# Attention and a gated MLP on one core: another written order of all operations, and another choice of engine for the movable ones

## The chip, the cores and the metric

The kernel runs on one core of a Trainium2 chip. Five instruction streams run side by side on that core: TensorE (PE, with its weight loads shown as PEld), VectorE (DVE), ScalarE (ACT), GpSimd (POOL) and SyncE (SP), which issues most of the DMAs. Each stream takes its own instructions strictly in the order in which they are written, and the streams wait for each other at semaphores. The metric is the device time of one execution in microseconds (us). Three runs of the kernel before gave a median of 943.7 us (943.67 to 944.27).

## The reference

Batch 8, 8 heads, 576 queries, head width 64. Keys and values are averaged over groups of 8 positions, so that 72 keys are left, and after the attention an MLP with a sigmoid gate runs over 4608 tokens.

```python
k_p = k.reshape(B, H, Sp, 8, D).mean(axis=3)      # Sp = 72
v_p = v.reshape(B, H, Sp, 8, D).mean(axis=3)
scores = scale * q @ k_p^T ; scores -= max
attn = exp(scores) / (sum(exp(scores)) + 1e-9)
x = (attn @ v_p), heads side by side              # 4608 x 512
h = x @ w_in                                      # 4608 x 2048
g = h * sigmoid(1.702 * h)
out = g @ w_out                                   # 4608 x 512
```

All inputs and the output are float32.

## The kernel before

**Work.** A batch's 576 tokens are cut into a chunk of 512 and 64 left over; the left-over tokens of all 8 batches make a ninth chunk (c = 8), gathered through DRAM. Batch b's attention makes the input of chunk b. Per batch: DMA keys and values, pool them on DVE (`red`, `kbd`, `vbd`, L747, L889), bring the queries in transposed 32-blocks (`qr`, `qt`), scores on PE (`sps`, L1148), maximum and subtraction on DVE (`nm`, `sc`, L1171, L1179), exp on ACT (L1200), sums and weighting (L1205, L1221), then the weights are rearranged by small copies of 32 rows (`tail` L1262, `main` L1271) and block transposes (`mt`, `tt`), split in a high and a low part (`ah`, `al`), and multiplied with the values (`pav`, L1406 to L1409). `pav` is copied to the chunk's `x` and to `xt` (L1448, L1451, L1460).

**Stages of the MLP.** At the start the weights come in as raw words and are decoded (`raw`, `e`, `w`, L1586 to L1633) into a high and a low float32r half. Chunks 0 and 1 are computed densely (`h`, L1693 to L1695; `g`, `gh`, `gl`, L1710 to L1723; `o`, L1735 to L1737). Chunks 2 to 8 use a seven-product form of a 2x2 block product, in f16 pieces: for each of 8 pairs p of hidden tiles the banks `ha` and `hb` take seven products (L1982), ACT and DVE copy, add and gate them (L1997, L2005, L2017), and the gated tiles are split into `gh` and `gl` (L437/L440 and L2043, or on POOL L2048 and L2051).

**The fold.** That form needs other weights. While chunk 1 runs, `fold` renews both weights: high and low half are added (L1774, tiles `stage` and `shared`), scaled (L437 on ACT or L440 on DVE, tile `t`), added and subtracted against each other (L1818, tile `stage`), and cut into an f16 high part (L1756) and the rest (L1759). The first weight's pieces go to DRAM (`wd`) and come back pair by pair (`ws`); the second's stay in place (`t1`).

**What sets the order.** The kernel first records every operation as a task, with its engine, what it reads and what it writes, and nothing is issued. Many tasks are movable: a copy may run on ACT or DVE, a SBUF-to-SBUF sum on POOL or DVE; a task then carries both forms. At the end a table of 4871 numbers, `ORDER`, is read from left to right; each number is the place of a task in the record, a negative one (-n-1) means that the task is issued on its other engine:

```python
for n in map(int, ORDER.split()):
    t = tasks[n if n >= 0 else -n - 1]
    if n < 0:
        t.swap()
    t.emit()
```

DMAs are tasks too, so the table also sets the order of SP's queue. The waits at semaphores follow from what the tasks read and write.

Of the kernel before, what the change touches and what calls it, by code (L numbers as in the profile page):

```python
# [42 lines left out]
3 0 2074 2075 2076 2077 2078 2079 2080 2081 2082 2083 2084 11 169 170 171 10 162 163 4 31 164 73 172 165 12 7 -168 32  # L43
-169 176 177 6 5 25 178 179 26 27 72 8 2 1 45 50 33 166 34 51 46 204 205 206 -182 23 24 52 47 35 2085 17 228 9 14 13
36 53 48 49 54 207 2086 183 184 185 29 40 41 30 37 38 229 230 231 42 43 39 44 2087 2088 2089 2090 155 57 156 157 55
173 65 16 15 18 19 20 21 68 56 58 67 66 59 60 64 74 97 61 63 62 -76 182 208 158 186 159 160 187 161 180 98 190 191 77
-77 69 -79 70 99 82 83 192 100 101 212 209 213 214 -175 22 107 84 102 -104 85 197 108 198 92 79 2091 87 104 88 112 215
28 -81 81 -94 86 199 451 268 252 449 220 300 244 308 448 284 450 456 236 260 457 292 324 276 458 340 459 418 417 416
415 316 269 270 109 89 105 271 106 94 113 253 254 90 114 255 117 91 110 95 221 96 115 111 116 232 175 200 193 2094
2095 2096 2097 2098 2099 2100 2101 188 189 222 194 223 -203 -196 216 203 2092 2109 2110 2111 2112 2113 2114 2115 119  # L50
2102 2103 2104 245 201 118 120 121 122 127 128 246 196 123 124 2116 -130 2107 136 130 125 -132 -138 247 -211 126 -212
2108 2105 2117 2118 218 237 238 261 138 132 2106 2119 2120 239 224 139 262 135 217 226 233 -134 134 219 2124 142 2122
2125 2126 -142 140 263 277 278 -235 -236 279 240 227 248 225 143 309 310 249 2127 2128 2129 148 144 2130 2131 2132
2133 -150 -243 301 302 280 -146 311 -251 -148 452 146 2123 150 303 264 2134 2218 2219 2220 421 151 152 422 285 286 287
419 2221 2121 2222 2223 2224 2225 293 241 294 295 2226 2227 312 251 243 -267 -268 272 256 -259 -260 71 288 2135 2136
2137 2139 2140 2141 2142 2143 2144 2145 2146 2228 2138 341 342 281 265 257 372 348 364 356 388 -154 460 343 420 -283
-284 428 427 429 430 332 296 325 273 326 2147 2148 313 327 2093 2229 425 2230 2233 2234 2235 2236 2237 2238 2239 2231
426 2240 2149 298 299 328 -275 2152 453 2232 2150 297 357 358 359 275 2151 317 2241 318 -2243 314 333 319 454 -291 433
466 464 473 396 467 472 475 465 434 474 404 431 432 334 289 -316 -2244 335 344 360 291 468 455 2154 2155 2156 2157
2158 2153 2159 2160 469 2248 2249 2161 2250 2251 2252 2244 2253 2254 435 470 304 306 -308 471 2162 329 -2164 336 305  # L60
2164 349 350 -331 476 351 2245 461 2255 2246 462 365 366 320 -323 463 367 2247 352 331 345 2256 2257 346 446 2165 477
2169 2170 2171 2172 2173 2174 2175 2166 2176 2167 2168 523 518 516 439 515 438 380 603 154 526 517 525 524 321 353 373
-324 436 447 478 -348 479 2258 374 2177 375 -339 -2179 424 389 390 -363 391 440 480 481 482 337 368 339 2179 2259 2261
2263 2264 2265 2266 2267 2268 2269 2180 2181 2182 2270 2260 405 361 406 407 483 519 527 441 442 2184 2183 376 363 2185
2186 2187 2188 2189 2190 2191 2271 2272 381 382 541 589 532 539 534 604 540 531 533 588 392 437 -445 445 2273 377 484
2262 486 487 489 383 -355 485 488 490 2274 2276 2278 2279 2192 2193 520 2280 355 -379 -380 384 370 397 398 521 522
2275 497 2281 399 535 2282 2277 -499 423 499 2194 393 385 -395 2293 536 537 2294 2295 2296 2283 491 2284 2285 2286
2195 395 2197 -493 493 538 -372 528 2297 494 2287 369 644 641 642 542 643 605 606 386 495 543 529 443 530 400 2288 387
408 409 402 2199 2200 2201 503 2202 496 -505 505 544 545 645 546 547 2203 2204 2291 506 2298 2299 2300 2205 2206 509
2292 2198 2196 590 -411 -404 411 401 2207 2208 2209 -511 511 548 -508 508 2289 512 2290 513 500 501 2301 2302 549 2308  # L70
2309 2310 2311 2214 514 552 550 502 551 2215 553 2312 2303 558 607 -560 560 412 556 554 654 592 639 591 2306 2304 2313
2314 2210 2315 565 2211 2323 2316 2317 593 555 -567 567 557 2324 561 2307 2325 2326 2327 2328 572 562 594 -2319 563
587 -565 -574 574 619 613 637 612 638 610 620 611 568 2321 -596 598 571 599 609 -570 575 -579 570 608 576 577 2329
2330 2331 601 2305 2342 579 413 636 -2333 -2334 2343 2319 2353 2354 -581 614 616 581 615 -601 582 2322 583 2338 2344
2320 2334 584 640 -2527 -598 414 602 585 2216 596 617 2335 2212 2339 2345 2355 2356 -619 2346 2347 646 2348 621 658
659 651 625 652 624 656 657 653 2357 2336 2358 2340 647 -2528 649 648 623 650 622 -635 -2547 660 2550 2530 -2532 655
626 627 2359 2364 2365 2366 2367 2352 2350 2351 2349 2360 661 662 -2548 2537 -2539 663 629 -2549 2368 2369 2536 2540
2363 2375 2386 2361 2376 2377 2378 630 2362 664 665 666 631 667 668 669 -2529 -675 2539 2541 2370 2374 2371 2542 -687
-2567 -2544 -689 628 -633 -671 2551 2556 729 734 2372 2387 2373 2388 2379 2380 735 730 2557 -2553 -2554 -2550 -678
-672 676 -2559 -2560 2381 680 679 685 2397 2389 2384 2398 2383 2382 2544 2545 682 689 -684 694 -676 -679 -2571 -691  # L80
2390 2391 -692 681 2419 2399 2385 2420 2400 727 733 2554 728 -2564 732 673 2560 731 -2687 2561 2392 2564 2401 672 2402
2571 -2578 736 697 2567 -2577 2568 693 2580 -693 -688 -685 -2579 -2533 698 2403 2396 2421 2394 2408 2409 2395 2422
2410 2411 2393 737 2405 2406 2407 2404 2581 695 2412 2413 2414 696 -2580 748 2562 750 2565 743 745 742 747 -2591 749
744 -2584 -2573 738 -2585 699 746 2582 740 -2592 -701 739 701 -2607 2585 2555 2529 2573 2533 2535 2569 884 847 2575
2423 2424 751 741 706 2416 2417 2430 2431 2432 2433 2441 2418 2442 752 2415 2425 2597 2586 -2588 -2599 2710 633 753
754 755 756 2607 -2597 -2601 2592 2434 2435 2436 2599 -2604 -2691 2601 2534 2602 831 887 2574 846 882 2429 2426 2443
2428 2427 2437 2444 757 2445 2446 -2611 2611 2687 -2712 -2695 -2594 758 -2696 -2617 2588 2604 2605 2617 2447 2618
-2620 -2699 -2631 2438 2452 2453 2439 2454 2440 2463 2464 2465 2455 2456 2620 707 2457 2696 2626 2450 2466 2448 2451
# [2488 lines left out]
```

## Time and profile before

| What | us |
|---|---|
| median of 3 runs | 943.7 (943.67 to 944.27) |
| the profiled execution's own time | 940.6 |
| span from its first to its last instruction | 938.6 |
| PE busy in the span | 863.9 (92%) |
| DVE busy | 788.4 (84%) |
| ACT busy | 541.8 (58%) |
| POOL busy | 400.6 (43%) |

The profiled execution took 2.0 us more than its span, and 3.1 us less than the median. A whole-span share hides the stages. The kernel's products set good marks: chunk 0's first product starts at 39.9 us, chunk 1's at 157.2, the pairs of chunk 2 at 277.5, of chunk 3 at 389.7, of chunk 4 at 477.3, of chunk 8 at 837.0. The stretches between these marks are read one by one below.

### The profile page before, as it was taken

How to read it: one execution, taken by the hardware profiler on the slowest of the kernel's cores; microseconds unless marked ns; L12 is line 12 of the kernel's file. 1: busy time of each engine (PE TensorE's matmuls, PEld its weight loads, DVE VectorE, ACT ScalarE, POOL GpSimd, SP SyncE). 2: the span in 40 equal slices, each digit the busy share in tenths (PEclk: the TensorE clock that was granted, in tenths of full speed). 3: DMA queues.
4: the chain of work that ended last, by engine and by line, in shares of the span. 5: the costliest groups of instructions: out<-in, count | busy, mean ns of one | idle time of the engine just before them, and what ended most of it. 6: DMA issues, size and time to landing. Idle time of an engine off the chain costs nothing.

```text
span 938.6 us, 16098 instructions
## 1 busy us (share of the span) xinstructions
PE 863.9 (92%) x5614; PEld 640.5 (68%) x5614; DVE 788.4 (84%) x1597; ACT 541.8 (58%) x1121; POOL 400.6 (43%) x376
## 2 busy tenths in 40 slices
PE   7999999998867887999999999999998999999997
PEld 7878888876755554566666666666665766666884
DVE  5987988899999998999998888799978684557696
ACT  5876853454666666677545574657574635335452
POOL 2576741547767645553231145524313126512221
PEclk9999999999989988999999999999999999999999
DMA  9963321322336553346454335364351335356532
GB/s 281 360 205 104 87 51 44 96 78 95 109 110 202 163 151 105 89 131 186 130 141 130 107 89 156 108 192 114 92 161 52 102 124 196 108 158 201 164 106 64
DMA packets 151313, 125.32 MB, mean 134 GB/s; under 512 B 86336, under 2 KB 108352, under 8 KB 151232
## 3 DMA queue, kind: packets, MB, share of 16 engines
q1 hardware_dynamic: 146384, 115.52, 42.1%
q10 hardware_dynamic: 4848, 8.78, 2.5%
q8 instruction: 44, 0.72, 0.3%
q14 instruction: 37, 0.30, 0.1%
HBM read 102.76 MB, written 21.50 MB: 132 GB/s over the span
## 4 chain that ended last, share of the span: by engine, by line
PE 43%; DVE 37%; ACT 7%; issue 6%; DMA 3%; SPq 2%; POOL 1%; DVEq 0%; ACTq 0%; POOLq 0%
PE ha L1982 9%; PE hb L1982 7%; PE o L2274 4%; PE o L2272 4%; PE o L2273 4%; DVE main L1271 2%; PE sps L1148 2%; DVE slots L2005 2%; DVE sc L1221 2%; DVE tail L1262 1%; DVE stage L1818 1%; DVE qt L1132 1%; DVE al L1389 1%; DVE sc L1179 1%; DVE nm L1171 1%
## 5 line engine op out<-in xcount | busy, mean ns | idle before, releaser
L1982 PEld LDWEIGHTS <-ws 128*128 128x128 f16 x2016 | 196.5, 98 | 95.8 <-issue 37.0
L1982 PE MATMUL ha<-x,ws 128*128 128x256 f16 x1008 | 138.8, 274 | 19.9 <-ACT slots L2017 7.3
L1982 PE MATMUL hb<-x,ws 128*128 128x256 f16 x1008 | 132.7, 273 | 11.3 <-DVE slots L2005 10.8
L2274 PE MATMUL o<-t,glall 128*128 128x512 f16 x256 | 97.7, 381 | 0.4 <-DVE glall L2043 0.4
L2272 PE MATMUL o<-t,ghall 128*128 128x512 f16 x256 | 97.9, 383 | 0.0
L2273 PE MATMUL o<-t,ghall 128*128 128x512 f16 x256 | 97.6, 381 | 0.0
L2005 DVE TENSOR_TENSOR slots<-slots,hb 128x256 f32<-128x256 f32 x139 | 56.2, 412 | 33.4 <-PE hb L1982 27.0
L2048 POOL TENSOR_TENSOR slots<-slots,smalls 128x512 f32<-128x512 f32 (+1 forms) x40 | 40.5, 1013 | 96.0 <-ACT ghall L437 49.0
L2017 ACT ACTIVATE slots<-slots,smalls 128x256 f32<-128x256 f32 (+1 forms) x108 | 61.2, 576 | 34.3 <-DVE slots L2005 32.7
L1997 ACT COPY slots<-ha 128x256 f32<-128x256 f32 x97 | 35.7, 368 | 78.3 <-PE ha L1982 76.8
L1693 PE MATMUL h<-x,w 128*128 128x256 f32 (+1 forms) x192 | 65.7, 342 | 4.8 <-ACT gh L1715 3.8
L1694 PE MATMUL h<-x,w 128*128 128x256 f32 (+1 forms) x192 | 62.8, 327 | 1.4 <-DVE w L1633 0.9
L1723 POOL TENSOR_TENSOR gl<-g,gh 128x512 fp32r<-128x512 f32 x29 | 43.0, 1481 | 47.9 <-ACT gh L1715 41.6
L1695 PE MATMUL h<-x,w 128*128 128x256 f32 (+1 forms) x192 | 62.5, 326 | 0.0
L1148 PE MATMUL sps<-k,qt 128*128 128x144 f32 x320 | 48.8, 297 | 7.5 <-DVE sc L1179 4.1
L1389 POOL TENSOR_TENSOR al<-mt,ah 128x320 fp32r<-128x320 f32 (+1 forms) x23 | 18.9, 822 | 84.7 <-ACT ah L1385 49.2
L1148 PEld LDWEIGHTS sps<-k,qt 128*128 128x128 f32 x320 | 44.1, 196 | 11.7 <-issue 5.1
L1271 ACT COPY main<-sc 32x384 f32<-32x384 f32 (+2 forms) x100 | 45.7, 457 | 10.5 <-DVE sc L1221 5.2
L1982 PE MATMUL ha<-x,shared 128*128 128x256 f16 x336 | 45.7, 273 | 3.8 <-ACT slots L1997 3.0
L2272 PE MATMUL o<-t,slots 128*128 128x512 f16 x128 | 48.6, 380 | 0.0
L2273 PE MATMUL o<-t,slots 128*128 128x512 f16 x128 | 48.6, 380 | 0.0
L2274 PE MATMUL o<-t,slots 128*128 128x512 f16 x128 | 48.6, 379 | 0.0
(396 smaller groups left out, 2340.4 us busy)
## 6 DMA issues: line engine op xcount, KB each, us to landing
ws<-wd SPq DMA_DIRECT2D x168, 256.0 KB
out_dram<-osb ACTq DMA_DIRECT2D x32, 256.0 KB
raw<-in_moe_w_in_dram SPq DMA_DIRECT2D x15, 512.0 KB
raw<-in_moe_w_out_dram SPq DMA_DIRECT2D x15, 512.0 KB
kv_False<-in_k_dram SPq DMA_DIRECT2D x28, 256.0 KB
kv_True<-in_v_dram SPq DMA_DIRECT2D x28, 256.0 KB
shared<-wd SPq DMA_DIRECT2D x56, 128.0 KB
qr<-in_q_dram SPq DMA_DIRECT2D x112, 40.0 KB
```

The source lines that it names most:

```text
L1148: nc.tensor.matmul(ps()[:, t * PW : (t + 1) * PW], lhsT=qt()[:, s0 : s0 + P], rhs=m.k2()[:, jj], start=True, stop=True,)
L1271: copy(out=main()[32 * r : 32 * (r + 1), :, cols].rearrange("p j t (k a) -> p t j a k", a=2), in_=sc()[rows, ts, :, 16 * r : 16 * (r + 1)] ...
L1693: nc.tensor.matmul(o, lhsT=w[:, 0, j], rhs=xs[:, 0], start=j == 0, stop=False)
L1694: nc.tensor.matmul(o, lhsT=w[:, 1, j], rhs=xs[:, 0], start=False, stop=False)
L1695: nc.tensor.matmul(o, lhsT=w[:, 0, j], rhs=xs[:, 1], start=False, stop=j == NJ - 1)
L1723: engine.tensor_tensor(out=gl(), in0=g(), in1=gh().bitcast(F32), op=ALU.subtract)
L1982: nc.tensor.matmul(o, lhsT=wv()[:, r, jj], rhs=xo(k, jj), start=start and n == 0, stop=n == len(terms) - 1,  skip_group_check=not start,)
L2005: lambda: nc.vector.tensor_tensor(out=part(i), in0=part(i), in1=hb()[:, half * 256 : half * 256 + 256], op=ALU.add),
L2017: lambda: nc.scalar.activation(out=out(), in_=src(), func=AF.Gelu_apprx_sigmoid, scale=inner()),
L2272: nc.tensor.matmul(o(), lhsT=gh()[:, tok], rhs=wp[:, 0], start=start, stop=False)
L2273: nc.tensor.matmul(o(), lhsT=gh()[:, tok], rhs=wp[:, 1], start=False, stop=False)
L2274: nc.tensor.matmul(o(), lhsT=gl()[:, tok], rhs=wp[:, 0], start=False, stop=stop)
```

## The change

Only the table `ORDER` is another: the same 4871 tasks, in another order throughout, and 709 of them on their other engine where 741 were before. The operations are the same. Its first two lines, before and after:

```diff
-3 0 2074 2075 2076 2077 2078 2079 2080 2081 2082 2083 2084 11 169 170 171 10 162 163 4 31 164 73 172 165 12 7 -168 32
--169 176 177 6 5 25 178 179 26 27 72 8 2 1 45 50 33 166 34 51 46 204 205 206 -182 23 24 52 47 35 2085 17 228 9 14 13
+2074 2075 2076 2077 9 155 156 157 10 162 163 164 165 158 2078 2079 2080 2081 2082 73 0 2083 2084 2085 2086 2087 2088
+2089 11 -161 169 170 171 4 6 3 31 1 5 22 159 72 166 172 173 32 25 26 33 7 8 50 2090 2 197 198 45 34 46 167 199 -52 52
```

Counted over the written order, in tasks (before, then after), between the marks named above:

| stretch | DVE | ACT | POOL |
|---|---|---|---|
| start to chunk 1 | 231, 225 | 179, 181 | 67, 63 |
| chunk 1 to chunk 2's pairs (the fold) | 175, 154 | 117, 141 | 61, 32 |
| chunk 2's pairs | 186, 180 | 128, 170 | 47, 38 |
| chunk 3's pairs to the end | 912, 919 | 606, 617 | 146, 133 |

In the fold's stretch the kinds that move between engines are: L1756 on DVE 14, then 2; L440 8, then 3; `main` L1271 14, then 8; `tail` L1262 9, then 4; L1759 on DVE 11, then 24 (on POOL 19, then 4); L1774 on DVE 16, then 20 (on POOL 9, then 6); L1818 on DVE 18, then 20 (on POOL 13, then 7).

The first place is POOL in the middle of chunk 1. `gl1_0_9` and the like are the low parts of chunk 1's gate for hidden tile 9 and so on (they stand on POOL in both orders), everything else is fold work or batch 2's attention. Before:

```order
L1723 TENSOR_TENSOR gl1_0_9_2554<-g1_0_9_2532,gh1_0_9_2534 128x512
L1818 TENSOR_TENSOR stage_2049<-stage_1955,t0_8_2486 128x256
L1774 TENSOR_TENSOR stage_2043<-w0_10_1043 128x512
L1723 TENSOR_TENSOR gl1_0_10_2616<-g1_0_10_2592,gh1_0_10_2597 128x512
L1818 TENSOR_TENSOR stage_2043<-t0_10_2626,t0_11_2621 128x256
L1759 TENSOR_TENSOR t0_6_2475<-t0_6_2475 128x512
L1389 TENSOR_TENSOR al2_0_1_2681<-mt2_0_1_2429,ah2_0_1_2595 128x256
L1723 TENSOR_TENSOR gl1_0_11_2683<-g1_0_11_2624,gh1_0_11_2632 128x512
L1759 TENSOR_TENSOR stage_2043<-stage_2043 128x512
L1759 TENSOR_TENSOR t1_0_2539<-t1_0_2539 128x512
L1723 TENSOR_TENSOR gl1_0_12_2738<-g1_0_12_2702,gh1_0_12_2704 128x512
```

and after, at the same place on POOL:

```order
L1723 TENSOR_TENSOR gl1_0_9_2570<-g1_0_9_2566,gh1_0_9_2568 128x512
L1818 TENSOR_TENSOR stage_1919<-t0_9_2555 128x256
L1723 TENSOR_TENSOR gl1_0_10_2617<-g1_0_10_2592,gh1_0_10_2594 128x512
L1723 TENSOR_TENSOR gl1_0_11_2672<-g1_0_11_2647,gh1_0_11_2655 128x512
L1723 TENSOR_TENSOR gl1_0_12_2738<-g1_0_12_2721,gh1_0_12_2735 128x512
L1723 TENSOR_TENSOR gl1_0_13_2856<-g1_0_13_2743,gh1_0_13_2747 128x512
L1759 TENSOR_TENSOR t1_1_2468<-t1_1_2468 128x512
L1723 TENSOR_TENSOR gl1_0_14_2887<-g1_0_14_2879,gh1_0_14_2884 128x512
```

Most of the fold's sums have left POOL here.

The second place is ACT in the pairs of chunk 2, from the exp of batch 3's first piece (`sc3_0`) on: `tail3_0` and `main3_0` are that batch's rearranged attention weights, `slots`, `gall` and `ghall` the tiles of chunk 2's gate. Before:

```order
L1200 ACTIVATE sc3_0_3350<-sc3_0_3350 128x1152
L1997 COPY slots12_3043<-ha2_4_3521 128x256
L2017 ACT_TABLE_LOAD
L2017 ACTIVATE slots14_3240<-slots14_3240,smalls_94 128x512
L1997 COPY slots15_3059<-ha2_4_3521 128x256
L1262 COPY tail3_0_3504<-sc3_0_3350 32x2x32
L1271 COPY main3_0_3507<-sc3_0_3350 32x2x4x2x16
L1083 CAST vh3_3578<-vbd3_3312 128x512
L1997 COPY slots15_3059<-ha2_4_3521 128x256
L1271 COPY main3_0_3507<-sc3_0_3350 32x2x4x2x16 x2
L437 ACTIVATE ghall_3209<-slots14_3240,smalls_94 128x512
L2017 ACTIVATE slots15_3059<-ha2_4_3521,smalls_94 128x256
```

and after, from the second copy of `ha2_5` on:

```order
L1997 COPY slots15_3056<-ha2_5_3589 128x256
L1083 CAST vh3_3622<-vbd3_3421 128x512
L1089 CAST vt3_3638<-tbd3_3181 96x512
L1262 COPY tail3_0_3646<-sc3_0_3390 32x2x32
L1271 COPY main3_0_3631<-sc3_0_3390 32x2x4x2x16
L1262 COPY tail3_0_3646<-sc3_0_3390 32x2x32 x2
L1271 COPY main3_0_3631<-sc3_0_3390 32x2x4x2x16
L437 ACTIVATE ghall_3190<-slots12_3045,smalls_94 128x512
L1271 COPY main3_0_3631<-sc3_0_3390 32x2x4x2x16 x4
L437 ACTIVATE ghall_3190<-slots15_3056,smalls_94 128x512
L1271 COPY main3_0_3631<-sc3_0_3390 32x2x4x2x16 x4
L1997 COPY gall_3077<-ha2_5_3589 128x256
```

ACT now has 10 of the 16 `main` copies of this piece where it had 6, and 6 of the 8 `tail` copies where it had 2; most of them stand ahead of a copy out of bank `ha2_5`.

The third place is the head of SP's queue, the loads of the first batch. Before:

```order
L622 DMA kv_150<-in_k_dram 128x1x512
L1555 DMA raw_179<-in_moe_w_in_dram 128x4x256
L1555 DMA raw_185<-in_moe_w_out_dram 128x1024
L622 DMA kv_150<-in_k_dram 128x1x512
L1555 DMA raw_205<-in_moe_w_out_dram 128x1024
L2162 DMA q_0_207<-in_q_dram 128x8x64
L683 DMA tl_217<-in_k_dram 64x8x64
L683 DMA tl_217<-in_v_dram 64x8x64
```

and after:

```order
L1555 DMA raw_159<-in_moe_w_in_dram 128x4x256
L1555 DMA raw_165<-in_moe_w_out_dram 128x1024
L1555 DMA raw_203<-in_moe_w_in_dram 128x4x256
L622 DMA kv_211<-in_k_dram 128x1x512
L683 DMA tl_213<-in_k_dram 64x8x64
L622 DMA kv_211<-in_k_dram 128x1x512
L622 DMA kv_225<-in_k_dram 128x1x512
L683 DMA tl_213<-in_v_dram 64x8x64
L1555 DMA raw_228<-in_moe_w_in_dram 128x4x256
L2162 DMA q_0_247<-in_q_dram 128x8x64 x2
```

The first query tile moves from the sixth place to the tenth, and three raw weight tiles stand ahead of the first keys where none did.

## Rows read from the trace of the kernel before

**Rows 1.** Page: busy tenths in 40 slices of 23.5 us, DMA rate.

```profile
PE   7999999998867887999999999999998999999997
...
DVE  5987988899999998999998888799978684557696
...
GB/s 281 360 205 104 87 51 44 96 78 95 109 110 202 163 151 105 89 131 186 130 141 130 107 89 156 108 192 114 92 161 52 102 124 196 108 158 201 164 106 64
```

**Rows 2.** The page: shares of the chain that ended last, by engine.

```profile
PE 43%; DVE 37%; ACT 7%; issue 6%; DMA 3%; SPq 2%; POOL 1%; DVEq 0%; ACTq 0%; POOLq 0%
```

**Rows 3.** Windows: length, busy us (instructions) by engine, clock, DMA share, rate.

```profile
0.00:157.20 157.20, 144.63 (x918) 128.24 (x919) 132.36 (x247) 107.28 (x221) 82.15 (x73) 0.98 0.55 169
63.50:157.20 93.70, 89.34 (x572) 79.61 (x571) 81.88 (x139) 61.01 (x127) 52.33 (x42) 0.98 0.28 71
157.20:277.50 120.30, 105.46 (x467) 85.24 (x465) 113.08 (x187) 64.53 (x122) 72.38 (x60) 0.96 0.31 92
277.50:389.70 112.20, 92.03 (x596) 63.05 (x595) 105.98 (x201) 71.83 (x144) 65.22 (x57) 0.94 0.50 140
389.70:940.00 550.30, 521.82 (x3639) 364.00 (x3636) 437.00 (x964) 298.20 (x637) 180.86 (x186) 1.00 0.44 131
```

**Rows 4.** PE's waits from 157 to 390 us: total, times, longest.

```profile
PE pav L1406 <- DVE x L1451: 6.9, 3, 4.5
PE ha L1982 <- ACT slots L2017: 6.1, 1, 6.1
```

**Rows 5.** DVE by form, 157 to 280 us: busy us, mean ns.

```profile
L1774 DVE TENSOR_TENSOR stage<-w 128x512 f32<-128x512 f32 x11 | 11.1, 1009 | 0.1
L1774 DVE TENSOR_TENSOR shared<-w 128x512 f32<-128x512 f32 x5 | 5.7, 1135 | 0.0
L440 DVE TENSOR_SCALAR t<-stage,smalls 128x512 f32<-128x512 f32 x6 | 4.8, 807 | 0.0
L1759 DVE TENSOR_TENSOR t<-t 128x512 f16<-128x512 f32 x4 | 4.5, 1141 | 0.0
L1818 DVE TENSOR_TENSOR stage<-t,stage 128x256 f32<-128x256 f32 x4 | 4.2, 1047 | 0.1
...
L1756 DVE CAST stage<-stage 128x512 f16<-128x512 f32 x6 | 3.8, 654 | 0.1
L1818 DVE TENSOR_TENSOR stage<-t,t 128x256 f32<-128x256 f32 x5 | 3.8, 750 | 0.0
L1818 DVE TENSOR_TENSOR stage<-t 128x256 f32<-128x256 f32 x3 | 3.4, 1131 | 0.0
L1818 DVE TENSOR_TENSOR stage<-stage,t 128x256 f32<-128x256 f32 x6 | 3.4, 563 | 0.1
...
L1271 DVE COPY main<-sc 32x256 f32<-32x256 f32 x9 | 2.6, 287 | 0.2
...
L1759 DVE TENSOR_TENSOR stage<-stage 128x512 f16<-128x512 f32 x3 | 2.2, 736 | 0.0
```

**Rows 6.** DVE's timeline, 200 to 212 us: start, us.

```profile
203.93 0.38 DVE L1818 TENSOR_TENSOR stage<-t,t 128x256 f32<-128x256 f32 x1
...
205.25 1.28 DVE L1818 TENSOR_TENSOR stage<-stage,t 128x256 f32<-128x256 f32 x1
...
209.84 0.68 DVE L1774 TENSOR_TENSOR stage<-w 128x512 f32<-128x512 f32 x1
210.44 0.41 DVE L1756 CAST stage<-stage 128x512 f16<-128x512 f32 x1
```

**Rows 7.** POOL's timeline, 200 to 212 us.

```profile
205.03 1.23 POOL L1759 TENSOR_TENSOR stage<-stage 128x512 f16<-128x512 f32 x1 [1.74 <-ACT stage L1756]
```

**Rows 8.** DVE by form, whole span.

```profile
L440 DVE TENSOR_SCALAR xt<-xt,smalls 128x512 f32<-128x512 f32 x4 | 1.9, 477 | 0.0
```

**Rows 9.** ACT's timeline, 352 to 368 us.

```profile
359.05 0.37 ACT L1460 COPY xt<-pav 128x256 f32<-128x256 f32 x1 [6.79 <-DVE x L1451]
```

**Rows 10.** PE's timeline, 354 to 367 us.

```profile
365.57 1.44 PE L1982 MATMUL ha<-x,ws 128*128 128x256 f16 x6 [6.08 <-ACT slots L2017]
```

406 rows, old and new, of the table ORDER are left out of this document.

## The prediction

> **What bounds the kernel now.** I read the page first. In the slices DVE stands at 8 and 9 tenths from about 210 to 350 us, and there PE falls to 6 to 8, while from 380 us on PE is at 9 nearly throughout [rows 1]. The chain that ended last is 43% PE and 37% DVE; the other engines hold little of it [rows 2]. So there are two kinds of stretch, and I cut the span at marks of the program with the windows view [rows 3]. Up to 157.2 us PE is busy 144.6 us. From 157.2 to 277.5, while chunk 1 runs and the weights are folded, DVE is busy 113.1 of 120.3 us and PE 105.5: PE idles 14.8 us. In the pairs of chunk 2, to 389.7, DVE is busy 106.0 of 112.2 and PE 92.0: PE idles 20.2. From there to the end PE is busy 521.8 of 550.3, DVE only 437.0. Two neighbouring stretches thus hold 35 of PE's 75 idle us, in a quarter of the time, and the view of waits says for whom: PE waits there for DVE's `x` (6.9 us in three waits) and once 6.1 us for ACT's gate [rows 4]. That one is DVE's too: ACT had idled 6.79 us behind a copy `xt` that waited for DVE's `x` [rows 9], did an exp after it, and the gate that PE's 6.08 us wait ended with came only then [rows 10].
>
> The same sums cost DVE very different times in the fold's stretch. A sum `stage` of 256 columns took 0.38 us at 203.93 and 1.28 us at 205.25 [rows 6], and the second lies inside a POOL sum that ran from 205.03 for 1.23 us [rows 7]. So DVE's busy time contains waiting for POOL. How much: take 0.38 for L1818, 0.68 for L1774 and for L1759 at 512 columns (the same size), 0.41 for L1756 [rows 6] and 0.48 for L440 [rows 8], against what the groups took [rows 5]:
> 16 L1774: 16.8 - 10.9 = 5.9. 18 L1818: 14.8 - 6.8 = 8.0. 7 L1759: 6.7 - 4.8 = 1.9. 6 L440: 4.8 - 2.9 = 1.9. 6 L1756: 3.8 - 2.5 = 1.3.
> Together 19.0 us, beside 60 POOL instructions [rows 3]: 0.32 us of DVE for each. Small copies and splits are not in this sum, so it is a lower bound.
>
> **The change part by part.** PE's work is the same; it ends sooner only if what feeds it does.
>
> *The fold's stretch.* POOL's tasks fall from 61 to 32. 29 x 0.32 = 9.2 us less waiting. What DVE does is exchanged: it takes 13 L1759 (8.8 us at 0.68), 4 L1774 (2.7) and 2 L1818 (0.8), 12.3 together; it gives away 12 L1756 (4.9), 5 L440 (2.4), 6 `main` copies (1.7 at the 0.287 of rows 5), 5 `tail` copies (1.4, taken at the same price), and some ten other single tasks, four of them transposes `mt`, for which I take 0.4 each, 4.0: 14.4. Net -2.1. DVE's need is then 113.1 - 9.2 - 2.1 = 101.8, and with the 7.2 us that it idles now 109.0. PE's is 105.5 and, with the idle share that it has from 63.5 to 157.2 (4.4 on 89.3, 4.9% [rows 3]), 110.7. So PE becomes the later of the two, and the stretch takes some 110.5 instead of 120.3: -9.8. ACT takes 24 tasks more, some 12 us at half a us each, and goes from 64.5 to 77 of 110: it stays in the shade of PE as long as nothing urgent stands behind its casts. Bounds: nothing (the four `mt` and what hangs on them only moved past the mark) and -14.8 (all of PE's idle time).
>
> *Chunk 2's pairs.* POOL 47 to 38 tasks, at the same price -2.9 us. DVE loses about 26 copies at 0.3 to 0.4 (-9) and takes some twenty longer operations, fewer in number but at 0.4 to 0.7 (+10.5). Net -1.4; since DVE fills 106.0 of 112.2, I count it in full: -1.5. Bounds -10 (half of PE's idle) and +9 (the slower rival below). ACT gains 42 tasks: some 16 us on 71.8 of 112.
>
> Row first, then rule: beside POOL one sum took 0.90 us longer, inside a POOL sum of 1.23 [rows 6, 7]. The Trainium skill, SBUF — State Buffer, section "SBUF: two separate sides", says that the read and write ports which DVE shares with GpSimd are an exclusive lock held for a whole instruction, against a DVE operation with two SBUF inputs or in a two-port mode. By that rule a DVE operation that comes at any moment would wait half a POOL instruction, 0.6 us (72.38 over 60 [rows 3]), not 0.32; the fold's stretch would be PE's all the same, chunk 2's would gain 4 instead of 1.5, and the sum would be -13.8, 930 us. The trace agrees with the lock, but not every POOL instruction meets such an operation; I stay with 0.32.
>
> *The start.* On SP's queue three raw tiles of 512 KB stand ahead of the first keys, and the first query tile has 3.0 MB ahead of it instead of 2.0. At the first slice's 281 GB/s [rows 1] that is 3.7 us later for the queries and some 2 us for the keys. The same raw tiles feed ACT and POOL sooner, PE idles 12.6 us before chunk 1 anyway [rows 3], and 4 POOL tasks fewer give 1.3 back. I take 0; bounds -2 and +4.
>
> *From 389.7 on.* DVE 912 to 919 tasks, ACT 606 to 617, POOL 146 to 133. DVE's own work grows by what POOL gave up, 13 x 0.68 = 8.8, less 13 x 0.32 = 4.2 of waiting: +4.6 on 437.0 of 550.3, beside a PE that is busy 95% of the time. It is hidden behind PE: 0. If that cover is gone here and there it costs the 4.6; another order may also open or close some of PE's 28.5 us of idle time: bounds -6 and +8.
>
> Sum: -9.8 - 1.5 + 0 + 0 = -11.3. The profiled execution took 940.6 (span 938.6 and 2.0 around it), so 929.3; the median of the runs is 3.1 above it: 932.4. I predict 932.
>
> **The rivals.**
> *A larger gain.* PE's busy time need not be its floor. In both stretches the granted clock is 0.96 and 0.94 [rows 3]; 105.5 x 0.96 = 101.2, with 4.9% idle 106.2: -14.1. In chunk 2's pairs DVE without any idle time needs 106.0 - 2.9 = 103.1: -9.1. That makes 943.7 - 23.2 = 920.5. For it: the clock is 1.00 from 389.7 on, where PE idles little [rows 3]. Against it: nothing removes all of DVE's waits for ACT. The Trainium skill, Perfetto Trace Analysis, section "Identifying the Most-Contended Engine", warns that a busy share of matmuls does not tell how near TensorE is to its limit, since pipelined matmuls look different in a trace; by it my bound of 110.7 is soft on this side.
>
> *Moved, not saved.* Part of batch 2's tail (four `mt`, and with each an `ah`, an `al` and copies of `pav`, some 2.2 us of DVE at these prices) stands behind the mark now. 8.8 us of the 9.8 would then be paid in chunk 2's pairs, where DVE is full. Time: 943.7 - 2.5 = 941, within a few us. For it: chunk 2's pairs wait for `x` [rows 4]. Against it: the waiting for POOL that goes is not moved anywhere.
>
> *Slower: ACT becomes late in chunk 2's pairs.* One mechanism: ACT takes its rows in order, and 10 `main` and 6 `tail` copies of batch 3's piece now stand around the copies out of `ha` and the gates that free PE's banks. A head-of-line wait of that kind cost PE 6.08 us once [rows 10]. Three more of them cost 18.2, less the 11.3 gained: +6.9, 950.6. It decides from two such waits on. For it: ACT goes to 88 of 112 us there, and each copy can only start when DVE's `sc` is done. Against it: ACT idles 36% of this stretch now, and the copies removed from DVE are what PE's `x` stood behind.
>
> **How the numbers follow.** Forecast 0.48 (924 to 940); larger gain 0.14; moved 0.12, of which 0.10 falls within 0.2% of 943.7 (1.9 us, about what a measurement of this kernel tells from no change) and 0.02 below; slower 0.26. Faster 0.48 + 0.14 + 0.02 = 0.64, same 0.10, slower 0.26. The range reaches from the larger gain with a good start and late part (920.5 - 3, 917) to the slower rival's 951; below lies some 0.05, above 0.12.
>
> **What would show it.** Right: in the same windows, the fold's stretch 110 us with PE idle near 5 and POOL near 40 busy; L1818 and L1774 on DVE with means nearer 0.5 and 0.8 than now; chunk 2's pairs 108 to 112 us; from chunk 3 on 550 within 5. A waits view in which PE's waits for DVE's `x` shrink. Wrong: a fold's stretch over 116 us; sums on DVE as slow as before although POOL does half; PE waits for ACT's L1997 and L2017 of over 15 us in chunk 2's pairs; chunk 0's first product over 3 us later than 39.9 with no return by chunk 1.

## The result, and the profile after

The changed kernel took 909.9 us, median of 4 runs (908.9 to 912.0), beside 943.7 for the kernel before: ratio 0.9651, 95% interval 0.9623 to 0.9678. The gain is 33.8 us where 11.3 were forecast, and the time lies below the range. The profiled execution took 908.9 us, its span is 907.0.

The page's slices of PE and DVE and its chain by engine, as in [rows 1, 2]:

```profile
PE   7999999998889888998999899999999999999997
...
DVE  6999988879889979998687988999988666555787
...
PE 42%; DVE 31%; ACT 12%; DMA 6%; issue 5%; SPq 3%; POOL 1%; ACTq 0%; DVEq 0%; POOLq 0%
```

Between the first slice and the last PE has none under 8 tenths any more, and DVE's share of the chain fell from 37% to 31%, while ACT's rose from 7% to 12%. The same stretches as in [rows 3], cut at the same marks (length, then busy us and instructions of PE, PEld, DVE, ACT, POOL, then clock, DMA share, rate):

```profile
0.00:145.00 145.00, 138.49 (x906) 123.59 (x907) 124.39 (x239) 110.34 (x226) 74.95 (x69) 0.99 0.58 179
145.00:259.60 114.60, 104.88 (x474) 86.22 (x472) 96.37 (x182) 79.92 (x155) 42.37 (x35) 0.96 0.37 110
259.60:360.80 101.20, 89.94 (x598) 63.43 (x598) 92.69 (x182) 79.30 (x171) 46.36 (x42) 0.98 0.51 144
360.80:907.00 546.20, 522.32 (x3642) 364.67 (x3640) 436.30 (x970) 301.89 (x652) 158.22 (x163) 1.00 0.45 132
```

| stretch | before | after | difference | forecast |
|---|---|---|---|---|
| start | 157.2 | 145.0 | -12.2 | 0 |
| fold | 120.3 | 114.6 | -5.7 | -9.8 |
| chunk 2's pairs | 112.2 | 101.2 | -11.0 | -1.5 |
| rest | 548.9 | 546.2 | -2.7 | 0 |

The differences add up to 31.6 us, that of the two spans; the medians are 33.8 apart because that of before stands 3.1 us above its profiled execution and that of after 1.0. Of the 31.6 us, 28.9 come before chunk 3. In the start half of the gain is idle time of PE (12.6 to 6.5 us) and half its busy time (144.6 to 138.5). DVE is busy 8.0, 16.7 and 13.3 us less in these three stretches, although it issues nearly as many instructions in all (1571 for 1597). DVE's rows by form in the fold's stretch, beside [rows 5] (busy us, mean ns, idle before):

```profile
L1774 DVE TENSOR_TENSOR stage<-w 128x512 f32<-128x512 f32 x12 | 10.0, 841 | 0.1
L1759 DVE TENSOR_TENSOR stage<-stage 128x512 f16<-128x512 f32 x10 | 6.9, 686 | 0.1
...
L1774 DVE TENSOR_TENSOR shared<-w 128x512 f32<-128x512 f32 x8 | 5.4, 682 | 0.0
...
L1818 DVE TENSOR_TENSOR stage<-t,stage 128x256 f32<-128x256 f32 x5 | 3.8, 768 | 0.1
...
L1818 DVE TENSOR_TENSOR stage<-stage,t 128x256 f32<-128x256 f32 x5 | 2.0, 410 | 0.4 <-ACT t L437 0.3
```

The same sums are shorter: 1009 and 1135 ns became 841 and 682, 1047 became 768, 563 became 410. To add this up over all of DVE I took for each line and form the 10th percentile of its durations in the two traces as its time alone, and call what a record has above it its excess. DVE's excess is 120.9 us in the trace of before and 77.3 in that of after; its work without excess went from 739.7 to 748.5. By stretch: start 18.5 to 12.5, fold 36.2 to 16.2, chunk 2's pairs 20.3 to 9.5.

Where it sat differs by stretch. In the start it was mostly the decoding of the weights (L1626, L1633): 10.7 us of excess before, 4.0 after. In chunk 2's pairs half of it was on copies of 32 rows (L916, L1262, L1271): 37 of them took 19.1 us of DVE, 9.7 of that excess; after, 18 took 6.5, 1.8 of it excess, and ACT has the others. Two of their rows, first before, then after:

```profile
L916 DVE COPY k<-kbd 32x128 f32<-32x128 f32 x9 | 5.9, 652 | 0.2
L1262 DVE COPY tail<-sc 32x64 f32<-32x64 f32 x6 | 3.1, 520 | 0.1
```

```profile
L916 DVE COPY k<-kbd 32x128 f32<-32x128 f32 x2 | 0.4, 220 | 0.1
L1262 DVE COPY tail<-sc 32x64 f32<-32x64 f32 x2 | 0.4, 185 | 0.0
```

PE's waits from 145 to 361 us, beside [rows 4]:

```profile
PE pav L1406 <- DVE x L1451: 6.0, 2, 4.8
PE sps L1148 <- DVE sc L1179: 2.5, 1, 2.5
PE ha L1982 <- ACT slots L1997: 2.4, 1, 2.4
```

The wait of 6.1 us for ACT's gate is gone, that for `x` is not.

### The profile page after: what moved, and what is told of

It is laid out like the page before. It is cut to its first block, busy times and chain, and to the rows that moved or that the text cites. A ratio compares the mean times of both kernels' runs of the same rounds, so it can differ in the third digit from the quotient of the medians.

```text
span 907.0 us, 16076 instructions
## 1 busy us (share of the span) xinstructions
PE 855.6 (94%) x5614; PEld 637.9 (70%) x5614; DVE 749.7 (83%) x1571; ACT 571.5 (63%) x1202; POOL 321.9 (35%) x307
## 4 chain that ended last, share of the span: by engine, by line
PE 42%; DVE 31%; ACT 12%; DMA 6%; issue 5%; SPq 3%; POOL 1%; ACTq 0%; DVEq 0%; POOLq 0%
PE ha L1982 9%; PE hb L1982 6%; PE o L2272 4%; PE o L2274 4%; PE o L2273 4%; ACT main L1271 3%; PE sps L1148 2%; ACT slots L2017 2%; DMA raw<-in_moe_w_in_dram 2%; DMA ws<-wd 1%; DVE slots L2005 1%; PE o_P L2502 1%; DVE nm L1171 1%; DVE qt L1132 1%; DVE sc L1179 1%
## 5 line engine op out<-in xcount | busy, mean ns | idle before, releaser
L1982 PE MATMUL ha<-x,ws 128*128 128x256 f16 x1008 | 137.6, 272 | 13.7 <-ACT slots L1997 3.6
L1982 PE MATMUL hb<-x,ws 128*128 128x256 f16 x1008 | 132.4, 273 | 5.5 <-DVE slots L2005 3.7
L1997 ACT COPY slots<-ha 128x256 f32<-128x256 f32 x94 | 34.7, 369 | 88.6 <-PE ha L1982 86.4
L2017 ACT ACTIVATE slots<-slots,smalls 128x256 f32<-128x256 f32 (+1 forms) x108 | 61.4, 577 | 34.8 <-DVE slots L2005 33.5
L1693 PE MATMUL h<-x,w 128*128 128x256 f32 (+1 forms) x192 | 63.2, 329 | 1.0 <-ACT g L1710 0.6
L1271 ACT COPY main<-sc 32x384 f32<-32x384 f32 (+2 forms) x117 | 53.0, 453 | 15.5 <-DVE mt L1378 6.1
L1723 POOL TENSOR_TENSOR gl<-g,gh 128x512 fp32r<-128x512 f32 x23 | 31.0, 1347 | 87.0 <-ACT gh L1715 60.8
L1695 PE MATMUL h<-x,w 128*128 128x256 f32 (+1 forms) x192 | 61.2, 319 | 0.0
L1694 PE MATMUL h<-x,w 128*128 128x256 f32 (+1 forms) x192 | 61.1, 318 | 0.0
L2048 POOL TENSOR_TENSOR slots<-slots,smalls 128x512 f32<-128x512 f32 (+1 forms) x32 | 33.6, 1050 | 61.2 <-ACT ghall L437 20.2
L1389 POOL TENSOR_TENSOR al<-mt,ah 128x256 fp32r<-128x256 f32 (+1 forms) x20 | 17.6, 882 | 98.4 <-ACT ah L1385 39.8
```

The lines of the kernel that those rows point to most:

```text
L1271: copy(out=main()[32 * r : 32 * (r + 1), :, cols].rearrange("p j t (k a) -> p t j a k", a=2), in_=sc()[rows, ts, :, 16 * r : 16 * (r + 1)] ...
L1693: nc.tensor.matmul(o, lhsT=w[:, 0, j], rhs=xs[:, 0], start=j == 0, stop=False)
L1694: nc.tensor.matmul(o, lhsT=w[:, 1, j], rhs=xs[:, 0], start=False, stop=False)
L1695: nc.tensor.matmul(o, lhsT=w[:, 0, j], rhs=xs[:, 1], start=False, stop=j == NJ - 1)
L1982: nc.tensor.matmul(o, lhsT=wv()[:, r, jj], rhs=xo(k, jj), start=start and n == 0, stop=n == len(terms) - 1,  skip_group_check=not start,)
L1997: t = copy(256, lambda copy: copy(out=part(i), in_=bank()[:, 0:256]), [bank], [at(i)])
```

## The experiments

Two theories ran through them. The hold: DVE's records contain waiting for POOL, and the change took some of it away. The queues: the gain lies in where operations stand, whatever the engines do to each other. Each expectation spells out what it means by its letters, and a letter holds for its group of runs. All ratios are to the kernel before on the same chip (its medians were 941.2 to 942.8).

### One half of the change alone (e1 to e4)

```diff
 # ORDER: for the 4871 tasks
-sequence of before, engines of before
+e1: sequence of after,  engines of before
+e2: sequence of before, engines of after
+e3: sequence of before, engines of after only for the 241 tasks that leave or join POOL
+e4: after's table up to chunk 1's first product, then before's for what is left
```

> The new written order, every task on the engine that it had before. Theory P (what is gained is DVE's waiting for POOL, since POOL has 55 sums fewer): the waiting stays, DVE's busy time stays over 780 us, and the time is 935 to 948. Theory O (the order feeds PE better, whatever the engines): 915 or less, most of the 34 us.

> The old written order, every task on the engine of the changed kernel. Theory P: DVE's busy time falls to about 750 us as in the changed kernel, and the time to 910 to 925. Theory O: 938 or more, since each order is made for its own engines.

> The old order; only the 241 tasks that change between POOL and DVE take their new engine (148 leave POOL, 93 come), the 529 that change between DVE and ACT stay as before. Theory P: POOL near 322 us busy, the sums L1774 and L1818 on DVE some 0.3 us shorter in the mean, time 918 to 935. Theory A (the relief is ACT's taking 81 of DVE's copies): DVE is fuller than before, 943 or more.

> Order and engines of the changed kernel up to chunk 1's first product, of the kernel before from there on. If the start's gain is its own: chunk 1 begins at 145 instead of 157 and the time is 929 to 934. If it is work put off behind the mark: chunk 1 begins at 145 to 148, but the fold's stretch is longer by as much, and the time is 940 to 946.

Measured: e1 1014.0 us, ratio 1.0745 (1.0703 to 1.0787); e2 1051.0, 1.1137 (1.1097 to 1.1177); e3 1002.9, 1.0625 (1.0579 to 1.0671); e4 939.7, 0.9966 (0.9940 to 0.9992). Each part alone costs 62 to 110 us; whatever expected a gain from the order or from a choice of engine by itself falls. O for e2 and A for e3 named a loss and are met, by far more than the reason they give. DVE was busy 770.9 us in e1 and 757.7 in e2, less than the 788.4 of before, and the time still grew. The waits of PE in e2 (its line numbers are lower by one) are many short ones for copies out of its banks, and some for chunk 1's gate:

```profile
PE ha L1981 <- DVE slots L1996: 20.6, 15, 4.5
PE h L1692 <- ACT gh L1714: 16.1, 5, 8.6
```

The reading is that an operation given to another engine stands there at a place that was written for the first one, and holds what is behind it. So order and choice are one plan, neither can be priced alone, and these runs neither show nor refute the hold. e4 ran like the changed kernel until about 140 us; then DVE stood 3.58 us behind a transpose `qt` whose query tile was loaded later in the other table, PE waited 4.2 us for an `ah` behind it, and chunk 1 began at 153.8. It is inconclusive on the start, since the seam costs what it should measure.

### The hold by itself (e5, e13)

```diff
+for j in range(24): nc.vector.<form>(...)                 # alone
+for j in range(24): nc.vector.<form>(...); nc.gpsimd.tensor_tensor(128x512, other tiles)
```

> This kernel computes nothing of the reference: it is 24 VectorE instructions of one form in a row, alone and then again beside a row of GpSimd sums 128x512 f32 that touch no tile of theirs, for seven forms that stand in the fold's stretch. P (VectorE is held while GpSimd reads or writes, and that is what its instructions were long by): sum 128x512 0.67 us alone and 1.0 to 1.1 beside GpSimd, sum 128x256 0.41 and about 0.8, scaled copy 128x512 0.47 and 0.7, cast 128x512 to f16 0.41 and 0.5 to 0.55, copies of 32 rows 0.22 and 0.18 alone and 0.5 to 0.6, copy 128x256 out of PSUM 0.41 and 0.41 to 0.5; beside ScalarE copies every form as alone. W (the long records of before came from something else of that kernel, such as its DMAs or waits that the trace books as busy time): every form within 5% of its time alone. The forecast's price was 0.32 us of VectorE for each GpSimd sum; by P the added time over the count of GpSimd sums comes out above that, at 0.4 to 0.6.

DVE's and POOL's timelines of e5: start, us for the whole row of instructions. Of each DVE form the first row is alone, the second beside POOL; the last beside ScalarE copies. POOL's first row is alone.

```profile
23.04 14.53 DVE L41 TENSOR_TENSOR do<-a,b 128x512 f32<-128x512 f32 x24
38.32 35.83 DVE L41 TENSOR_TENSOR do<-a,b 128x512 f32<-128x512 f32 x24
...
179.94 3.33 DVE L53 COPY do<-a 32x128 f32<-32x128 f32 x24
184.25 16.33 DVE L53 COPY do<-a 32x128 f32<-32x128 f32 x24
...
222.07 8.03 DVE L59 COPY do<-bank 128x256 f32<-128x256 f32 x24
230.84 8.04 DVE L59 COPY do<-bank 128x256 f32<-128x256 f32 x24
...
249.15 14.54 DVE L41 TENSOR_TENSOR do<-a,b 128x512 f32<-128x512 f32 x24
```

```profile
7.50 14.68 POOL L62 TENSOR_TENSOR po<-c,d 128x512 f32<-128x512 f32 x12 [1.11 <-DMA d<-in_q_dram]
...
39.01 33.38 POOL L62 TENSOR_TENSOR po<-c,d 128x512 f32<-128x512 f32 x20
...
184.47 14.68 POOL L62 TENSOR_TENSOR po<-c,d 128x512 f32<-128x512 f32 x12
```

(35.83 - 14.53) / 20 = 1.07 us of DVE for each POOL sum. In the same way 1.06 for sums of 256 columns (23.03 - 8.13 over 14), 1.00 for scaled copies (25.65 - 9.59 over 16), 1.07 for casts (25.17 - 8.13 over 16), 1.08 for 32-row copies (16.33 - 3.33 over 12), 1.11 at 64 columns; 0.00 for copies out of PSUM, and 0.00 beside ScalarE. W falls, and even P's 0.4 to 0.6 for a GpSimd sum was too low by half. By the mean of its records a POOL sum takes 1.26 us alone and 1.70 beside DVE's sums of 512 columns: there the two engines take turns. Beside the 32-row copies twelve POOL sums took 14.68 us, as alone: there only DVE stands. Copies out of PSUM stay out of it.

> Computes nothing of the reference: rows of 24 VectorE instructions, alone and beside GpSimd, as before. L (while a GpSimd instruction reads or writes SBUF, a VectorE instruction that works on SBUF alone stands, whatever the GpSimd instruction is): a GpSimd copy 128x512, one input instead of two, holds VectorE for about its own length less 0.2 us. Sums 128x256 of one SBUF and one PSUM tile: 0.42 alone, and, if one PSUM operand is enough to be free, 0.42 beside GpSimd. Alternating copies of 32 rows (held) and copies out of PSUM (free): the copy of 32 rows takes the whole wait, so that the row is longer by 0.7 to 1.0 us a GpSimd sum. M (only two inputs on either side collide): GpSimd copies hold nothing.

```profile
14.17 23.60 DVE L41 TENSOR_TENSOR do<-a,b 128x512 f32<-128x512 f32 x24
...
39.77 8.36 DVE L44 COPY do<-a 32x128 f32<-32x128 f32 x24
...
57.77 8.02 DVE L47 TENSOR_TENSOR do<-a,bank 128x256 f32<-128x256 f32 x24
```

A POOL copy took 0.61 us alone and holds DVE for (8.36 - 3.33) / 12 = 0.42 beside copies of 32 rows and (23.60 - 14.53) / 24 = 0.38 beside sums of 512 columns; a DVE sum with one operand in PSUM took 8.02 us alone and beside POOL; in the row of alternating copies a POOL sum still costs 0.76 ((14.09 - 5.68) / 11). L holds, M falls.

### The choice undone, stretch by stretch (e6, e7, e9 to e11)

```diff
 # in the table of after, at the same places: e6 37 tasks of the fold, e7 20 of chunk 2's pairs,
 # e9 the start's 20 that concern POOL, e10 its other 50 (ACT and DVE), e11 all 70
-... -2671 ...        # a POOL task issued on DVE
+... 2670 ...         # the same task on POOL, as before
```

> The changed kernel with one thing undone: the 37 sums of the fold's stretch that it took from GpSimd to VectorE stand on GpSimd again, at the same places of the written order. P: VectorE loses 37 x 0.6 = 22 us of work in the stretch and gains 15 to 20 us by the added 41 us of GpSimd, so that its busy time stays within 8 us of 96, and the stretch grows by the wait for later results, 3 to 8 us of 114.6: 913 to 918 us, ratio 0.970 to 0.978. W (the relief of GpSimd is worth nothing, the order carries the gain): the sums are cheaper where another engine does them, the stretch stays at 114.6 within 2 us, 908 to 912. O (order and choice are one plan, so that any choice undone in its order jams queues): plus 15 us or more in the one stretch, above 925.

> The changed kernel with the 20 sums of the stretch of chunk 2's pairs (101.2 us long) that it took from GpSimd to VectorE put back on GpSimd, at the same places of the written order. P: plus 2 to 6 us, 912 to 916. W: within 2 us of 909.9. O: plus 10 us or more.

> The changed kernel with the 20 choices of the start (up to chunk 1's first product) that touch GpSimd put back: 12 sums back to GpSimd, 8 back to VectorE; the written order and the other 50 choices of the start stay. P (a GpSimd sum holds VectorE for most of its length, 1.0 to 1.1 us beside a dense row of VectorE work, as measured): net 4 sums more on GpSimd, about 4 us more of held VectorE, start 145.0 becomes 147 to 150, end 912 to 915. S (the start's 12.2 us come from where its operations are written and not from the choice): 145 within 1 us, 909 to 911. O (choice and order are one plan): 152 or more, above 917.

> The changed kernel with the other 50 choices of the start put back: 22 small operations from VectorE to ScalarE and 28 from ScalarE to VectorE; GpSimd's sums stay as changed. P: VectorE's work in the start changes by little, and no GpSimd sum moves: 145 within 2 us, 909 to 912. S: 145 within 1 us. O: the queues were filled for the other choice, an operation that comes late on one of them holds all behind it: 150 or more, above 915.

> Both of the last together: the changed kernel with all 70 choices of the start as before, in the changed order. S: the start stays at 145 within 2 us, 909 to 912. P: as with the 20 choices on GpSimd alone, 147 to 150. O: as far as the two add up or more, above 155, like the whole new order with the old choice, which was 157.5 there.

Measured: e6 920.5 (0.9762; 0.9745 to 0.9779), e7 923.5 (0.9796; 0.9774 to 0.9817), e9 915.3 (0.9713; 0.9685 to 0.9742), e10 917.1 (0.9739; 0.9710 to 0.9768), e11 922.4 (0.9781; 0.9750 to 0.9813). Each stretch in its own run, as in the windows above:

```profile
146.10:268.90 122.80, 104.73 (x473) 85.16 (x471) 88.39 (x144) 80.11 (x156) 85.36 (x72) 0.96 0.34 101
```

```profile
258.80:370.20 111.40, 94.58 (x599) 65.82 (x599) 90.09 (x164) 80.45 (x173) 76.59 (x70) 0.94 0.47 132
```

```profile
0.00:157.60 157.60, 141.71 (x905) 124.42 (x906) 126.17 (x242) 106.72 (x220) 82.94 (x75) 0.98 0.53 164
```

The fold is 8.2 us longer than after, chunk 2's pairs 10.2, the start 12.6 with all 70 choices undone (5.4 with the 20 and 8.5 with the 50). In the changed order, undoing these choices thus costs the start's whole gain (12.2), nearly all of the pairs' (11.0) and more than the fold's (5.7). S and W fall. P's upper ends were passed by 2.5 us in e6 and by 0.4 in e9; O's figures were met in e7, e10 and e11: small operations of ACT and DVE matter in the start beside POOL's (in e10 DVE is busy 132.4 us to its first product of chunk 1, 124.4 after; its excess is 17.5 for 12.5, with POOL's tasks as they were). The hold is there in e6 too: DVE's work without excess falls by 21.8 us in its stretch and the excess rises by 10.7, so that DVE is busy only 8.0 us less. But it is not shown to cost the time there, since PE waits for POOL's own late results, which stand behind the fold's sums in its queue; the longest wait, 8.0 us, is for a `gl` behind a sum `t` (L1759) that stood 6.91 us for ACT's cast:

```profile
PE o L1737 <- POOL gl L1723: 9.6, 3, 8.0
PE h L1693 <- ACT gh L1715: 7.3, 3, 5.0
```

The choices between ACT and DVE in the fold and in the pairs were not undone by themselves, so their share stays open.

### The hold made shorter, order and engines kept (e14 to e17)

In the kernel before, PE hardly waits for POOL in the two stretches from 157 to 390 us:

```profile
PE ha L1982 <- POOL x L1493: 0.3, 1, 0.3
PE o L1737 <- POOL gl L1723: 0.2, 1, 0.2
```

So there the hold can be taken down alone, nearly: POOL copies instead of POOL sums. What is computed is then no longer the reference's.

```diff
 # GpSimd's two-input instructions between two marks, nothing else
-    nc.gpsimd.tensor_tensor(out=out, in0=in0, in1=in1, op=op)
+    nc.gpsimd.tensor_copy(out=out, in_=in0)
```

> The kernel before with the 108 two-input instructions that stand on GpSimd from chunk 1's first product to chunk 3's pairs made copies of their first input: order, engines, and the work of VectorE, ScalarE and TensorE unchanged, the values are not the reference's. L: GpSimd's busy time in the two stretches, 137.6 us, falls by a third to a half, the 56.5 us by which VectorE's instructions are longer there than at their shortest fall in the same share, and since VectorE is busy 219 of 232.5 us there, the time falls by 8 to 17 us: 926 to 935. Q (the hold costs nothing that lasts, the gain of the change was in the places in the queues): within 3 us of 942.

> The same with the changed kernel: its 70 two-input instructions on GpSimd in the two stretches become copies of their first input. L: the 25.7 us of longer VectorE instructions fall by a third to a half; VectorE is busy 189 of 216 us here and no longer the fullest of the engines, so little of it is time: 0 to 5 us less, 905 to 910. Q: 908 to 912. If the same relief is worth as much here as in the kernel before, the hold was not what the change took away.

> The kernel before with the 67 two-input instructions that GpSimd has up to chunk 1's first product made copies of their first input; order, engines and all other work as before, the values are not the reference's. L: GpSimd's 82 us of the start fall to 40 to 50, VectorE's 18.5 us of longer instructions to 7 to 10, and chunk 1's first product comes 4 to 10 us sooner than 157.2, at 147 to 153; end to end 932 to 938. Q (the start waits for its loads and its queues, not for VectorE): 156 to 158, within 2 us of 942.

> The same with the 63 of the changed kernel. TensorE is busy there from 39 us on in all but 1.8 us, so L and Q both give little: chunk 1's first product at 143 to 145 for 145.0, 907 to 910. If the start shortens by more, TensorE's busy time in it was waiting too.

Measured: e14 911.7 (0.9689; 0.9671 to 0.9708), e15 903.6 (0.9596; 0.9569 to 0.9623), e16 934.2 (0.9921; 0.9895 to 0.9947; one of its five runs took 4957.6 us, the others 930.0 to 935.3), e17 909.9 (0.9664; 0.9640 to 0.9689). The windows of e14 (fold, pairs, rest), then of e16 (start), e15 (fold, pairs) and e17 (start):

```profile
157.40:259.60 102.20, 99.54 (x468) 82.09 (x468) 86.81 (x187) 64.25 (x122) 40.45 (x60) 1.00 0.36 107
259.60:360.10 100.50, 88.31 (x595) 62.75 (x595) 92.18 (x201) 71.56 (x144) 35.90 (x58) 0.98 0.56 157
360.10:908.00 547.90, 523.55 (x3639) 364.74 (x3636) 436.44 (x964) 298.18 (x637) 180.58 (x186) 1.00 0.45 131
```

```profile
0.00:147.60 147.60, 139.00 (x918) 124.68 (x919) 121.21 (x247) 106.39 (x221) 44.27 (x73) 1.00 0.60 180
```

```profile
144.20:252.10 107.90, 102.56 (x474) 84.62 (x473) 86.20 (x182) 79.75 (x155) 22.37 (x36) 0.97 0.40 119
252.10:349.30 97.20, 88.29 (x598) 62.07 (x598) 87.87 (x182) 78.71 (x171) 24.95 (x40) 1.00 0.52 147
```

```profile
0.00:143.60 143.60, 137.15 (x906) 123.44 (x907) 121.06 (x239) 109.90 (x226) 44.79 (x70) 0.99 0.60 181
```

| | start | fold | pairs | together |
|---|---|---|---|---|
| before | 157.2 | 120.3 | 112.2 | 389.7 |
| before, POOL shorter | 147.6 | 102.2 | 100.5 | 350.3 |
| after | 145.0 | 114.6 | 101.2 | 360.8 |
| after, POOL shorter | 143.6 | 107.9 | 97.2 | 348.7 |
| DVE's excess, four values in the order of the rows above | 18.5, 7.1, 12.5, 9.6 | 36.2, 9.5, 16.2, 5.6 | 20.3, 6.3, 9.5, 4.7 | 75.0, 22.9, 38.2, 19.9 |

The rows with POOL shorter take the start from one run (e16, e17) and the other two stretches from another (e14, e15); no run had both. Read it by rows: with the same order, the same engines and the same DVE instructions, the kernel before becomes 39.4 us shorter up to chunk 3 when POOL holds DVE less, more than the changed kernel did (28.9). The changed kernel becomes 12.1 us shorter by the same means. With the hold cut down the two plans differ by 1.6 us instead of 28.9. Both then stand near PE's own busy time (326.9 of 350.3 and 328.0 of 348.7 us), so smaller differences between the plans may be hidden there. End to end e14 gains 29.5 us, e16 7.7, e15 some 6 and e17 nothing; e15's last stretch, from chunk 3 on, was 6.2 us longer than the changed kernel's (552.4 for 546.2), and why is open.

Q falls in e14, e15 and e16. L is right in direction, and e16 and e17 lie within its figures; e14 and e15 went past them. L let the excess fall by a third to a half, like POOL's busy time (137.6 to 76.4 us in e14); it fell from 56.5 to 15.8. In the fold PE was also granted a clock of 1.00 instead of 0.96, and in e16's start, with the same 918 instructions, PE's busy time fell from 144.6 to 139.0 us. One thing is not separated: a copy also ends sooner than a sum. ACT waited 12.1 us for POOL in the two stretches of before, most of it for `gl`, and 0.5 in e14.

### Two attempts to go further (e8, e12)

```diff
 # e8, at 240 us, all engines as they are: the copies out of pav ahead of nine copies main<-sc
-... -722 -785 722 -2720 -2668 770 771 777 765 781 2715 778 769 763 710 766 775 705 ... -704 -713 704 ... 711
+... 710 705 -713 -704 704 711 -722 -785 722 -2720 -2668 770 771 777 765 781 2715 778 769 763 766 775 ...
 # e12: 34 of POOL's remaining sums from 145 to 361 us, where their inputs are ready
-... 2693 ...
+... -2694 ...
```

> The changed kernel with its engines as they are and 13 operations moved forward at six places where TensorE waits 1.2 to 4.8 us for an instruction that was ready but stood behind others in its engine's queue: at 251 us the four copies and two differences out of the two pav banks in front of nine copies main<-sc, at 328 us one x<-pav in front of a key reduction, at 295 us a slots<-hb in front of two long VectorE sums, at 346 us a gl sum in front of the weighing product, at 549 us a slots<-hb in front of a cast and a difference, at 631 us a left<-pav in front of two casts. They are 12.8 us of TensorE's 51.4 us of idle time (with the second pav wait of 1.2). Q (what is left of the idle time is the place in a queue): half to three quarters of that comes back as time, 900 to 904 us. R (another engine is as late, the wait only moves): 908 to 912.

> The changed kernel with 34 of the 49 sums that GpSimd still has in the fold's stretch and in chunk 2's pairs, and that VectorE can do, moved to VectorE, each written where its inputs were ready. By the price measured by itself (a GpSimd sum of 1.26 us holds a dense VectorE for 1.0 to 1.1 us, and VectorE does the same sum in 0.67) VectorE's busy time in the two stretches, 189 us, does not grow, or falls by up to 10 us, and the time falls by 1 to 5 us: 905 to 909. By the forecast's price of 0.32 a sum, VectorE's busy time grows by 34 x 0.35 = 12 us and the time by 2 to 8 us: 912 to 918. If a sum that VectorE must do in its order comes late and holds what is behind it, more than 918.

e8 took 910.3 us (0.9647; 0.9617 to 0.9678): no change. The wait of 4.8 us for `pav` is gone, and PE waits for the next late thing, in e8:

```profile
PE o L1735 <- ACT gh L1715: 4.3, 1, 4.3
```

That is R. e12 took 922.3 us (0.9777; 0.9756 to 0.9798). Its two stretches:

```profile
147.70:264.40 116.70, 103.45 (x473) 84.25 (x471) 100.21 (x194) 80.07 (x156) 32.35 (x25) 0.97 0.37 109
264.40:373.90 109.50, 92.44 (x598) 63.92 (x598) 103.56 (x205) 79.40 (x172) 21.09 (x18) 0.97 0.47 133
```

POOL is busy 35 us less, DVE 14.7 more, its excess falls by only 3.7: 0.11 us for a sum. The measured 1.07 is the price beside a dense row of SBUF work; that the sums which the change left on POOL stand mostly beside other work is the likely reason, and no run shows it. So a single price does not plan this kernel, and no version here that computes the reference beats the changed one.

## Why the prediction was wrong

**The failed step is the term for DVE's waiting for POOL, 0.32 us for each POOL task that goes.** The text called the price a lower bound, since small copies and splits were not in it, and then stayed with it. It took 9.2 us less waiting in the fold, 2.9 in chunk 2's pairs and 1.3 in the start; DVE's excess fell there by 20.0, 10.8 and 6.0. The mechanism was right and its size was not. By itself a POOL sum costs DVE 1.00 to 1.11 us beside SBUF work and nothing beside work on PSUM. In the trace of before, the excess is 36.2 us over 60 POOL instructions in the fold (0.60), 20.3 over 57 in the pairs (0.36) and 18.5 over 73 in the start (0.25); the five groups that the text summed held 20.0 of the fold's 36.2. Among what was left out are the 32-row copies, hit hardest for their size: 0.14 us apart in a row of their own, 1.08 more for each POOL sum. (The text's example, the sum of 1.28 us at 205.25, begins inside the POOL sum and ends 0.27 us after it.)

**The second fault goes with it: the price was applied to the count of POOL tasks that go, so that little could come where the count stays.** These are the two terms with the largest misses. The start was costed at 0 on its loads and on 4 POOL tasks fewer; it gained 12.2. With POOL's instructions shortened in the old plan it gains 9.6 (e16). Chunk 2's pairs were costed at -1.5 for 9 tasks fewer and 26 copies that leave DVE at 0.3 to 0.4 us; they gained 11.0, and 11.7 with POOL shortened in the old plan (e14). The copies of 32 rows had a mean of 0.52 there, half of it excess (19.1 and 9.7 us of 37). What counts is also what DVE does while POOL runs: in e10 the excess of the start grew by 5.0 us with no POOL task moved. That the new order itself lowered it is likely, and no run separates it from the choice.

**Against the 0.32 stood a second price, half a POOL instruction (0.6 us), which the text worked out and set aside.** It would have given 930 us, nearer by 2 and still 20 too long. The Trainium skill, SBUF — State Buffer, section "SBUF: two separate sides", says that the pair of ports is locked for a whole instruction and the loser stands. e5 agrees: one POOL sum of 1.26 us held a dense row of DVE for 1.00 to 1.11, most of its length and not half.

**The fold** was forecast at -9.8 and came to -5.7, with the mechanism right: POOL's busy time 72.4 to 42.4, near the 40 named, and DVE's further down (96.4) than the 101.8 forecast, although its work without excess, forecast at -2.1, rose from 84.7 to 88.7. The step that failed there is PE's idle share of 4.9%: PE idles 9.7 of 114.6 us, 6.0 of it for `x`, which stood behind copies on ACT in the longer of the two waits (4.8). e14's fold, with 2.7 us idle, shows that so small a share is possible there.

**The rest** came to -2.7, within its bounds of -6 and +8. The slower rival (ACT late at PE's banks) did not come: PE's waits for ACT's L1997 and L2017 in chunk 2's pairs are under 3 us, where over 15 would have shown it. "Moved, not saved" falls too, since the pairs got shorter. The larger gain (920.5) was the nearest, though it named the fold for the most of it.

## What to carry to other kernels

Look at the same instruction form at its shortest and at its mean: here the mean of 32-row copies was up to three times that of rows nearly free of excess (652 ns for 220), and much of DVE's busy time was waiting for POOL. The sum of the excess was a better measure of what there is to gain than a price per task: 40.7 us less of it gave 29.8 us in e14's two stretches, 11.4 less gave 9.6 in e16's start. Test it by making POOL's instructions shorter without moving anything; here that showed in two runs what the parts of the change could not. An order and a choice of engines that were planned together are judged together: each part alone cost 62 to 110 us.

## What the runs showed of the hardware

GpSimd held even VectorE's single-input copies of 32 rows (0.14 us apart alone, 0.68 beside sums), while one operand in PSUM was enough to be free (8.02 us for 24 sums of 256 columns, alone and beside POOL). A GpSimd copy of 128x512 held VectorE 0.38 to 0.42 us, a sum 1.00 to 1.11. GpSimd was slowed by VectorE's sums of 512 columns (1.26 us a sum alone, 1.70 beside them) and not by the copies of 32 rows (12 sums in 14.68 us, alone and beside them). In the fold, with the same instructions, PE idled 14.8 us at a granted clock of 0.96 before, and 2.7 at 1.00 in e14; its busy time fell from 105.5 to 99.5 us, a third of that stretch's gain.
